# Order of the first four attention units on TensorE: own values, the next unit's scores, then the carried values, then transposes and k^T v

## Chip, cores, metric

One core of one Trainium2 chip. The metric is device time in microseconds (us); lower is better. Every time below is the median of several executions, with the range. Ratios are of means; where an interval holds 1, the ratio alone shows no difference.

Names: PE is TensorE's matmul, PEld its weight load, ACT ScalarE, DVE VectorE, POOL GpSimd, SP SyncE.

## The reference

Retention attention (scores with a decay, causal, without softmax) for 8 batches and 8 heads of 576 tokens and 64 dimensions, then a mixture of 4 experts over all 4608 tokens, mixed by given probabilities:

```python
scores = scale * np.matmul(q, k.transpose(0, 1, 3, 2))
ret = scores * Dmat[None]                 # gamma_h ** (i - j) for i >= j, else 0
attn = np.matmul(ret, v)                  # (8, 8, 576, 64) -> x (4608, 512)
for e in range(4):
    h = np.maximum(x @ w1[e], 0.0)
    out += p[:, e:e + 1] * (h @ w2[e])
```

The experts are nearly all of the work. Attention of batch 0 has to be done before the first expert product can start; attention of later batches is woven in between expert products.

## The kernel before

Batch 0 is cut into four units (two halves of the tokens, two groups of four heads). One unit goes through these steps; the comments give the names used below:

```python
class Unit:
    def trans_pe(self, between=0):      # "transposes": k and q on PE, then one copy to qkT on ACT
        for i, n in ((1, "k"), (0, "q")):
            if i == 0 and between:
                warm(between)           # "fillers": matmuls of zeros, 512 columns each
            ...                         # 4 transposes of 128 columns
        nc.scalar.activation(self.qk..., pt..., Copy)
    def scores(self):                   # 16 matmuls of a quarter of the array (64 x 64),
        ...                             # then one product with the triangle on DVE: sT
    def kv(self):                       # "k^T v": 16 or 24 small matmuls,
        ...                             # then two copies to sbd on ACT, 64 partitions each
    def values_own(self):               # 16 quarter-array matmuls of v and sT into o
        ...
    def values_carried(self):           # 2 or 4 matmuls of sbd and qkT, added into the same o,
        ...                             # then two copies to xt on ACT
```

The order in which they are issued (numbers in the text are the unit numbers u = 0 to 3):

```python
for u in range(NU):
    if u + 1 < NU:
        us[u + 1].cast(...)             # k and q on DVE, v on POOL; loads of w1 for u + 1 in (1, 2)
    if u < NU - 1:
        us[u].scores()
        if u == 0:
            warm(4)
        us[u + 1].trans_pe(2 if u == 0 else 1)
        us[u].kv()
    if u == 0:
        warm(1)
    us[u].values_own()
    if u == NU - 2:
        us[u + 1].scores()
        us[u + 1].kv()
        us[u].values_carried()
        warm(3)
    else:
        us[u].values_carried()
# ... cut: then the first expert's up products, ph = w1^T x, which read xt
```

Products that fill PSUM share a ring of four tiles, and in the traces PE's matmuls run in the order of the program.

## Time and profile before

| | before |
|---|---|
| time, 3 executions | 542.52 us (542.24 to 542.67) |
| span of the profiled execution | 540.9 us |
| PE busy | 532.8 us, 98% |
| carried values 0 start | 11.50 us |
| last xt copy ends | 21.60 us |

The page's first part of the kernel before gives busy us, the share of the span and the number of instructions of each engine:

```profile
PE 532.8 (98%) x4319; PEld 341.3 (63%) x4319; DVE 365.4 (68%) x484; ACT 112.1 (21%) x255; POOL 91.8 (17%) x126
```

PE is the engine to watch, and from 21.7 us on it has next to no gaps. So the only place where an order can matter is the stage before. The chain of waits of the kernel before (what the end was waiting for, read backwards; columns: start us, us, what), from carried values 0 (o L602) on:

```profile
11.50 0.29 PE o L602 x2
11.79 0.35 PE s L539 x16
12.13 0.33 PE pt L516 x4
12.46 0.21 PE w L140
12.68 0.24 PE pt L516 x4
...
13.00 1.02 ACT qkT L518
14.02 0.36 ACT sbd L577
...
14.83 0.34 PE o L602 x3
15.18 0.35 PE s L539 x16
...
16.39 1.03 ACT qkT L518
...
17.46 0.41 PE s L539 x13
17.87 0.07 issue
17.94 0.25 PE s L539 x3
18.19 1.09 PE kvp L558 x24
...
20.09 1.21 ACT xt L618 x3
...
21.34 2.84 PE ph L358 x12
```

It runs back and forth between PE and ACT, with a period of 3.39 us (the qkT copies at 13.00 and 16.39). The scores (s L539) of the next unit stand in every round although nothing in the round needs them. At the end there are four xt copies in a row on ACT, because carried values 2 were issued after k^T v 3.

### The profile page before, as it was taken

How to read it: one execution, taken by the hardware profiler on the slowest of the kernel's cores; microseconds unless marked ns; L12 is line 12 of the kernel's file. 1: busy time of each engine (PE TensorE's matmuls, PEld its weight loads, DVE VectorE, ACT ScalarE, POOL GpSimd, SP SyncE). 2: the span in 40 equal slices, each digit the busy share in tenths (PEclk: the TensorE clock that was granted, in tenths of full speed). 3: DMA queues.
4: the chain of work that ended last, by engine and by line, in shares of the span. 5: the costliest groups of instructions: out<-in, count | busy, mean ns of one | idle time of the engine just before them, and what ended most of it. 6: DMA issues, size and time to landing. Idle time of an engine off the chain costs nothing.

```text
span 540.9 us, 10332 instructions
## 1 busy us (share of the span) xinstructions
PE 532.8 (98%) x4319; PEld 341.3 (63%) x4319; DVE 365.4 (68%) x484; ACT 112.1 (21%) x255; POOL 91.8 (17%) x126
## 2 busy tenths in 40 slices
PE   8999999999999999999999999999999999999997
PEld 4544454568745884488547864687448844884486
DVE  5525669987488657876688648764886677557764
ACT  4623551122111220223022111131112200000010
POOL 5734002120211121211112111112111100010000
PEclk9999999999999999999999999999999999999999
DMA  9999947765265635655277517653654211110001
GB/s 237 208 209 249 229 121 187 142 160 121 82 117 131 154 92 98 139 116 142 67 155 131 147 55 135 150 140 90 99 135 118 75 49 39 41 41 21 0 26 54
DMA packets 145119, 63.56 MB, mean 118 GB/s; under 512 B 124240, under 2 KB 135888, under 8 KB 145072
## 3 DMA queue, kind: packets, MB, share of 16 engines
q1 hardware_dynamic: 134752, 43.50, 35.7%
q0 software_dynamic: 10176, 19.27, 16.3%
q8 instruction: 34, 0.56, 0.4%
q10 hardware_dynamic: 144, 0.13, 0.1%
q14 instruction: 13, 0.11, 0.1%
HBM read 53.56 MB, written 9.51 MB: 117 GB/s over the span
## 4 chain that ended last, share of the span: by engine, by line
PE 92%; DVE 4%; ACT 1%; DMA 1%; issue 0%; SPq 0%; DVEq 0%; ACTq 0%
PE ph L358 44%; PE pd L450 37%; PE po L377 4%; DVE h L364 2%; PE kvp L261 1%; PE s L274 1%; PE o L291 1%; ACT qkT L518 1%; DMA raw_0q<-in_q_dram 1%; PE pt L516 1%; PE o L284 1%; PE s L539 1%; DMA qkT<-bf_q 0%; DVE sT L541 0%; PE kvp L558 0%
## 5 line engine op out<-in xcount | busy, mean ns | idle before, releaser
L358 PE MATMUL ph<-xt,w 128*128 128x512 bf16 x1152 | 255.3, 379 | 1.3 <-DVE h L364 1.2
L358 PEld LDWEIGHTS <-w 128*128 128x128 bf16 x1152 | 110.8, 98 | 129.4 <-issue 1.7
L364 DVE SCALAR_TENSOR_TENSOR h<-ph,pB 128x1024 bf16<-128x1024 f32 x128 | 155.9, 1222 | 51.8 <-PE ph L358 51.6
L450 PEld LDWEIGHTS <-h 128*128 128x128 bf16 x1024 | 99.2, 98 | 14.1
L450 PEld LDWEIGHTS <-s 128*128 128x128 bf16 x768 | 74.7, 98 | 9.1
L450 PE MATMUL pd<-wx,h 128*128 128x256 bf16 x512 | 61.3, 273 | 0.0
L450 PE MATMUL pd<-wx,s 128*128 128x256 bf16 x512 | 61.2, 273 | 0.0
L222 POOL DMA_DIRECT2D pB<-pd x28 | 15.9, 568 | 169.5 <-DVE h L364 137.7
L266 ACT ACTIVATE sbd<-kvp 64x256 bf16<-64x256 f32 x48 | 18.2, 378 | 106.4 <-PE kvp L261 106.1
L485 POOL TENSOR_TENSOR ob<-v,p 128x256 f32<-128x256 f32 x15 | 10.9, 727 | 151.1 <-DVE v L482 99.1
L276 DVE TENSOR_TENSOR sT<-s,tri 128x1024 bf16<-128x1024 f32 x24 | 29.2, 1216 | 2.1 <-PE s L274 2.1
L450 PE MATMUL pd<-t4w,h 128*128 128x256 bf16 x256 | 30.6, 273 | 0.0
L450 PE MATMUL pd<-t2w,s 128*128 128x256 bf16 x256 | 30.6, 273 | 0.0
L450 PE MATMUL pd<-t3w,h 128*128 128x256 bf16 x256 | 30.6, 273 | 0.0
L467 DVE TENSOR_TENSOR u<-pd,p 128x256 f32<-128x256 f32 x16 | 6.8, 425 | 34.5 <-PE pd L450 34.5
L245 POOL TENSOR_TENSOR bf_q<-raw_q,gq 128x512 bf16<-128x512 f32 x24 | 25.7, 1070 | 23.4 <-DMA raw_q<-in_q_dram 16.8
L377 PE MATMUL po<-wx,h 128*128 128x512 bf16 x128 | 29.1, 379 | 0.1
L458 ACT ACTIVATE p<-pd 128x256 f32<-128x256 f32 x16 | 6.1, 384 | 94.9 <-PE pd L450 90.8
L469 DVE TENSOR_TENSOR oa<-pd,u 128x256 f32<-128x256 f32 x16 | 6.8, 424 | 23.7 <-PE pd L450 23.7
L431 DVE TENSOR_TENSOR s<-h,s 128x1024 bf16<-128x1024 bf16 x32 | 22.7, 748 | 0.0
L241 DVE TENSOR_TENSOR bf_k<-raw_k,gk 128x512 bf16<-128x512 f32 x24 | 21.9, 912 | 0.0
L249 ACT ACTIVATE bf_v<-raw_v 128x512 bf16<-128x512 f32 x24 | 15.1, 628 | 29.8 <-DMA raw_v<-in_v_dram 29.8
(147 smaller groups left out, 392.2 us busy)
## 6 DMA issues: line engine op xcount, KB each, us to landing
pB<-pd POOLq DMA_DIRECT2D x28, 256.0 KB, 3.9
raw_k<-in_k_dram SPq DMA_DIRECT2D x48, 128.0 KB, 2.8
raw_q<-in_q_dram SPq DMA_DIRECT2D x48, 128.0 KB, 3.1
raw_v<-in_v_dram SPq DMA_DIRECT2D x48, 128.0 KB, 3.8
wx<-in_moe_w_dram POOLq DMA_DIRECT2D x4, 1024.0 KB, 15.3
out_dram<-oa SPq DMA_DIRECT2D x16, 256.0 KB, 2.1
out_dram<-ob SPq DMA_DIRECT2D x15, 256.0 KB, 2.1
w<-in_moe_w_dram POOLq DMA_DIRECT2D x3, 1024.0 KB, 15.6
```

The costliest lines, as they stand in the source:

```text
L222: eng.dma_start(out=pB[t, e], in_=pd[e:e + 1, t * NT:(t + 1) * NT].to_broadcast([128, NT]))
L241: nc.vector.tensor_tensor(self.bf["k"], raw["k"], gk[:, :, 2 * p:2 * p + 2].unsqueeze(3).to_broadcast([128, NC, 2, D]), op=MULT)
L245: nc.gpsimd.tensor_tensor(self.bf["q"], raw["q"], gq[:, :, 2 * p:2 * p + 2].unsqueeze(3).to_broadcast([128, NC, 2, D]), op=MULT)
L249: nc.scalar.activation(self.bf[n], raw[n], Copy)
L266: nc.scalar.activation(sbd[r, self.p, :, r], kvp[r, :, :], Copy)
L276: nc.vector.tensor_tensor(self.sT[:, :, :, :].rearrange("p j c t -> p (j c) t"), s[:, :, :, :].rearrange("p j c t -> p (j c) t"), tri[:, : ...
L358: nc.tensor.matmul(ph[:, f, :], lhsT=w1_sb[e][:, dc, fc * 128:(fc + 1) * 128], rhs=x[:, dc, :], start=(dc == 0), stop=(dc == NDC - 1))
L364: nc.vector.scalar_tensor_tensor(h[:, fk:fk + 2, :], ph, 0.0, pB[t, e][:, :].unsqueeze(1).to_broadcast([128, 2, NT]), op0=MAX, op1=MULT)
L377: nc.tensor.matmul(po[:, g, :], lhsT=h[:, e * NFC + fc, ns * 128:(ns + 1) * 128], rhs=wx[e // 2][:, (e % 2) * NFC + fc, :, :].rearrange("p ...
L431: nc.vector.tensor_tensor(self.alloc("s4")[:, l], h[:, r, self.a], self.s2[:, l], op=SUB)
L450: mm = nc.tensor.matmul(dst, lhsT=src[:, kk, tok], rhs=rhs(c), start=(start and c == 0), stop=(c == KH - 1), skip_group_check=True)
L485: nc.gpsimd.tensor_tensor(self.ob[:, HF:Dm], self.v, self.p5, op=ADD)
```

## The change

The intent: PE waits for the sbd copies ahead of each carried values. Put the next unit's scores, which are ready, into that wait, and start the transposes right after the carried values. One filler less is issued at the end.

```diff
+    cast_unit(1)
+    us[0].scores()
+    warm(4)
+    us[1].trans_pe(2)
+    us[0].kv()
+    warm(1)
     for u in range(NU):
-        ... (the loop shown above)
+        if u + 2 < NU:
+            cast_unit(u + 2)
+        us[u].values_own()
+        if u + 1 < NU:
+            us[u + 1].scores()
+        us[u].values_carried()
+        if u + 2 < NU:
+            us[u + 2].trans_pe(1)
+        if u + 1 < NU:
+            us[u + 1].kv()
         if u == NU - 2:
-            us[u + 1].scores()
-            us[u + 1].kv()
-            us[u].values_carried()
-            warm(3)
-        else:
-            us[u].values_carried()
+            warm(2)
```

So there are two parts: the scores move into the wait (units 0 and 1), and carried values 2 move ahead of k^T v 3 (the tail).

## The prediction

> **What bounds the kernel.** The page gives TensorE (PE) 532.8 of 540.9 us busy (98%). The timeline shows PE with almost no gap from 21.7 us to the end. What idles lies before that, where four units (quarters of batch 0) go round PE and ScalarE (ACT) before the first expert product (ph). The chain of waits there has a cycle of 3.39 us per unit: qkT copy on ACT 1.02, two sbd copies on ACT 0.76, carried values on PE 0.34, next unit's scores 0.35, transposes with one filler 0.78, hand-overs 0.14 (qkT 2 starts at 13.00, qkT 3 at 16.39). After the last copy (ends 17.42): scores 3, k^T v 3 (18.19 to 19.28), sbd copies (19.30 to 20.07), and then four xt copies on ACT to 21.60, two of them unit 2's, whose carried values stand behind unit 3's k^T v. ph starts at 20.64 but has to wait for the third and fourth xt copy (21.34, 21.65).

> **What the change does.** One filler matmul of 0.21 us goes, nothing is added. In the built programs VectorE, GpSimd and DMA keep their order; ACT swaps only unit 2's xt copies with unit 3's sbd copies. On PE the scores of unit u+1 move ahead of the carried values of u, into time in which PE waits for the sbd copies: 0.31 us before carried 0 and 0.36 before carried 1.

> **Costed on the chain.**
> 1. Scores (0.35) leave the cycle: carried 0 stays at 11.50, qkT 2 starts at about 12.65 (was 13.00), qkT 3 at about 15.7 (was 16.39). xt 0 and xt 1 (0.77) just fit beside the transposes (0.78).
> 2. Between qkT 3 and k^T v 3 there is now a wait for sbd 2 (0.76) and carried 2, where before there were slow scores 3 (0.73). That gives back 0.25: k^T v 3 starts at about 17.75 (was 18.19), sbd 3 at 18.85.
> 3. xt 2 is done by then (17.8 to 18.6). The tail after sbd 3 is carried 3 (0.34) plus two xt copies (0.77), with hand-overs 1.2, against four copies, 1.5, before. Gain 0.3.
> Sum: last xt copy at about 20.85 against 21.60, 0.75 us earlier. PE is dense from there on, so most of it should last.

> **What could take it back.** The first half of w2 landed at about 26.6 (GpSimd's wait that ended at 26.61); the first down product, which needs it, began at 27.9 and would begin at about 27.1: 0.5 us of slack is left. The clock: [...] (512-column fillers 0.43 us apart at first, 0.21 from 5.9 us on). I expect no gap over 0.45 us, so no slow-down from the missing filler.

> **Prediction.** 542.52 - 0.75 = about 541.8 us, 0.14% faster; 8 in 10: 541.3 to 542.4. Faster by over 2%: 0.005; within 2%: 0.99; slower: 0.005.

> **What shows it right or wrong.** qkT 2 and 3 starting 0.35 and 0.7 us earlier; k^T v 3 at about 17.75; PE waiting for sbd before carried 2; two, not four, xt copies at the end; ph dense from about 20.9; then the down product at 27.1. Wrong if PE is late on another wait (scores 3 then slow again), if VectorE's scores products (1.22 us each) come to bind own values.

## The result, and the profile after

541.54 us (541.31 to 541.59, 4 executions) against 542.54 us (542.24 to 542.67, 4 executions): 1.0 us, or 0.18%, less. The ratio of the kernels is 0.9982, 95% interval 0.9964 to 0.9999. (A ratio is the mean time of one kernel's executions over that of the other's in the same rounds, so not quite the ratio of the medians.) By the measure of 2% that is the same. A second set, c_after below, gave 541.50 us (541.25 to 542.74, 5 executions) against 542.45 us.

The page's first part of the changed kernel, and the groups of the ph matmuls, before and then after:

```profile
PE 528.9 (98%) x4278; PEld 340.8 (63%) x4318; DVE 366.4 (68%) x484; ACT 112.3 (21%) x255; POOL 92.8 (17%) x126
```

```profile
L358 PE MATMUL ph<-xt,w 128*128 128x512 bf16 x1152 | 255.3, 379 | 1.3 <-DVE h L364 1.2
```

```profile
L358 PE MATMUL ph<-xt,w 128*128 128x512 bf16 x1118 | 252.5, 379 | 3.3 <-DVE h L364 1.4
```

Do not read the fall of PE's busy time, 3.9 us, as the gain. The programs have the same 1152 ph matmuls, but this trace holds records of only 1118; only one filler was really removed (PEld: 4319 to 4318). The chain of waits of the changed kernel shows the stage itself:

```profile
11.09 0.30 PE o L602 x2
...
11.41 0.69 ACT xt L618 x2
...
12.15 1.02 ACT qkT L518
13.18 0.36 ACT sbd L577
...
13.99 0.35 PE o L602 x3
...
14.36 0.68 ACT xt L618 x2
...
15.09 1.03 ACT qkT L518
...
16.16 0.41 PE s L539 x13
16.57 0.48 issue
17.05 0.25 PE s L539 x3
17.30 0.22 PE o L602 x2
17.52 1.07 PE kvp L558 x24
...
19.84 0.47 ACT xt L618
...
20.34 3.71 PE ph L358 x16
```

The scores are gone from the round, whose period is now 2.94 us (12.15 to 15.09). The transposes have left the chain as well: the xt copies on ACT, which run beside them, now end last. At the end two xt copies are left instead of four. ph goes on at 20.34 us instead of 21.34. Two things in this trace are not what the change does:

- Carried values 0 start at 11.09 instead of 11.50 us, and up to own values 0 the two programs are the same; carried values 0 wait for the sbd copies, which do not depend on the scores now issued in between. So 0.41 of the 1.0 us between the traces was there before the change begins.
- The pause inside scores 3 is longer: 0.48 us on the chain, where the kernel before had 0.07.

### The profile page after: what moved, and what is told of

The parts are those of the page before. It is cut to its first block, busy times and chain, and to the rows that moved or that the text cites. A ratio compares the mean times of both kernels' runs of the same rounds, so it can differ in the third digit from the quotient of the medians. Undisturbed runs are those within 1.5% of the kernel's fastest.

```text
span 539.9 us, 10290 instructions
## 1 busy us (share of the span) xinstructions
PE 528.9 (98%) x4278; PEld 340.8 (63%) x4318; DVE 366.4 (68%) x484; ACT 112.3 (21%) x255; POOL 92.8 (17%) x126
## 3 DMA queue, kind: packets, MB, share of 16 engines
HBM read 53.56 MB, written 9.51 MB: 117 GB/s over the span
## 4 chain that ended last, share of the span: by engine, by line
PE 92%; DVE 4%; ACT 1%; issue 1%; DMA 1%; SPq 0%; DVEq 0%
PE ph L358 45%; PE pd L450 37%; PE po L377 4%; DVE h L364 2%; PE kvp L261 1%; PE s L274 1%; PE o L291 1%; ACT qkT L518 1%; DMA raw_0q<-in_q_dram 1%; PE o L284 1%; DVE sT L541 0%; PE kvp L558 0%; PE pt L516 0%; PE s L539 0%; PE o L602 0%
## 5 line engine op out<-in xcount | busy, mean ns | idle before, releaser
L358 PE MATMUL ph<-xt,w 128*128 128x512 bf16 x1118 | 252.5, 379 | 3.3 <-DVE h L364 1.4
L485 POOL TENSOR_TENSOR ob<-v,p 128x256 f32<-128x256 f32 x15 | 10.9, 727 | 146.9 <-DVE v L482 97.6
L245 POOL TENSOR_TENSOR bf_q<-raw_q,gq 128x512 bf16<-128x512 f32 x24 | 26.6, 1108 | 27.0 <-DMA raw_q<-in_q_dram 15.1
L429 DVE TENSOR_TENSOR h<-h 128x1024 bf16<-128x1024 bf16 x32 | 22.2, 735 | 0.0
```

Of the source, the lines that this page charges most:

```text
L245: nc.gpsimd.tensor_tensor(self.bf["q"], raw["q"], gq[:, :, 2 * p:2 * p + 2].unsqueeze(3).to_broadcast([128, NC, 2, D]), op=MULT)
L358: nc.tensor.matmul(ph[:, f, :], lhsT=w1_sb[e][:, dc, fc * 128:(fc + 1) * 128], rhs=x[:, dc, :], start=(dc == 0), stop=(dc == NDC - 1))
L429: nc.vector.tensor_tensor(h[:, l, self.b], h[:, l, self.a], h[:, l, self.b], op=SUB)
L485: nc.gpsimd.tensor_tensor(self.ob[:, HF:Dm], self.v, self.p5, op=ADD)
```

## The experiments

All times stand beside executions of the kernel before on the same chip. The table has what each trace shows: when PE reached full rate (by the clock record of the trace; the profile's clock column does not show this first change: it stands at 1.00 while fillers of 512 columns are still 0.43 us apart), when carried values 0 start, when the last xt copy ends, the difference of the two, which I call the stage, how far apart the two scores 3 matmuls are between which the pause falls (other neighbours in scores 3: at most 0.07 us), and the time of the profiled execution.

| trace | full rate from | carried 0 starts | last xt copy ends | stage | pause in scores 3 | time |
|---|---|---|---|---|---|---|
| before | 6.39 | 11.50 | 21.60 | 10.10 | 0.29 | 542.67 |
| c_before | 6.17 | 11.71 | 21.60 | 9.89 | 0.09 | 542.70 |
| after | 4.07 | 11.09 | 20.60 | 9.51 | 0.70 | 541.59 |
| c_after | 4.68 | 11.24 | 21.53 | 10.29, half clock from 18.3 | 0.56 | 542.74 |
| e_scores | 6.72 | 11.41 | 20.30 | 8.89 | none | 541.31 |
| e_tail | 5.00 | 11.42 | 21.41 | 9.99 | 0.10 | 542.85 |
| e_more | 5.27 | 11.29 | 20.37 | 9.08 | none | 541.45 |
| e_less | 4.08 | 11.01 | 22.25 | 11.24, half clock from 10.9 | none | 543.43 |
| e_split | 6.92 | 11.37 | 20.07 | 8.70 | 0.42 | 541.30 |
| e_nofill | 4.72 | 11.54 | 20.58 | 9.04, half clock from 18.4 | 0.17 | 543.10 |
| e_gap | 7.09 | 11.40 | 21.07 | 9.67 | 0.65 | 542.06 |
| e_pos | 4.03 | 11.10 | 20.18 | 9.08 | 0.19 | 541.16 |
| e_best | 7.00 | 11.24 | 20.30 | 9.06 | 0.56 | 541.52 |
| e_final | 4.03 | 11.63 | 19.91 | 8.28 | none | 541.13 |

In all rows but one the time is the end of the last xt copy plus 521.0 to 521.4 us (the exception, e_nofill, still runs at half clock when ph starts). So what is won or lost by 21 us is kept to the end, and the stage is all that has to be explained.

### Two controls: c_before and c_after

The two kernels again, unchanged, to see what differs between executions of one and the same program.

> Control: the kernel before, unchanged. All theories: within 0.3 us of the kernel before. Theory A (0.6 us of the 1.0 us gain belong to the new order; 0.4 us that the two traces differ by before carried values 0 is scatter of the start: when PE reached full rate and when the first q landed): over further traces the start of carried values 0 scatters between about 11.0 and 11.5 us for one and the same kernel, and copies of one kernel differ by up to 0.4 us. Rival B (the whole 1.0 us belongs to the change): this trace again has carried values 0 at 11.5.

> The changed kernel again, on the chip of the other runs. Theory A: 0.6 to 1.0 us below before, carried values 0 anywhere between 11.0 and 11.5 us, and the last xt copy 9.5 us after its start (10.1 in the kernel before). Rival B: 1.0 us below before and carried values 0 at 11.1 again.

c_before: 542.46 us (542.15 to 542.70) against 542.45 us, ratio 1.0001 (0.9989 to 1.0014). c_after: 541.50 us (541.25 to 542.74), ratio 0.9990 (0.9977 to 1.0002); one of its five executions, the profiled one, is at 542.74, and one at 542.03.

The start of carried values 0 does scatter: 11.01 to 11.71 us over all 14 traces, 11.09 to 11.71 over these two kernels, where the code up to there is the same. One part of it can be seen: the fillers at the start are 0.43 us apart until PE reaches full rate and 0.21 after, and that moment falls anywhere between 4.0 and 7.1 us; unit 0's transposes are slow or fast accordingly (four of them took 0.61 us in the kernel before, 0.40 in c_after). It does not explain all (e_final has an early one and the second latest carried values 0). Theory A, that the trace difference of 1.0 us is part change and part start, holds. But the start has no reason to favour one kernel over several executions, and the medians differ by 0.95 to 1.0 us in both sets. That suggests a stage that is on the average shorter than the first trace shows, and the pause in scores 3 is where the next runs found room.

### The two parts alone: e_scores and e_tail

```diff
 # e_scores: the changed kernel, with the old tail for unit 2
+        if u == NU - 2:
+            us[u + 1].kv()
+            us[u].values_carried()
+            warm(3)
+            continue
         us[u].values_carried()
 ...
```

```diff
 # e_tail: the kernel before, with the new tail for unit 2
             us[u + 1].scores()
-            us[u + 1].kv()
             us[u].values_carried()
-            warm(3)
+            us[u + 1].kv()
+            warm(2)
```

> New order for units 0 and 1 alone; unit 2 keeps the old tail (k^T v 3 ahead of carried values 2, three fillers, four xt copies at the end). If scores in the hand-over are the main part: qkT copy 3 starts 4.0 us after carried values 0, as in the changed kernel (4.9 before), the last xt copy ends about 9.65 us after it, and the time is 0.4 to 0.5 us below before, 0.1 to 0.2 above the changed kernel. If the tail is the main part: less than 0.2 below before.

> Old order for units 0 and 1, unit 2 with the new tail (carried values 2 ahead of k^T v 3, two fillers). qkT copy 3 starts 4.9 us after carried values 0 as before; k^T v 3 is later by about 0.25 as it now waits for the sbd copies 2 and carried values 2, which eats most of what two instead of four xt copies at the end give: the last xt copy ends about 10.0 after carried values 0, the time 0.1 us below before (0 to 0.2). If the tail is the main part: 0.3 or more below before.

e_scores: 541.67 us (541.31 to 543.13) against 542.45 us, ratio 0.9994 (0.9981 to 1.0008). One execution at 543.13 (clock 1.000, cause open) pulls its mean up; the other four, 541.31 to 541.70, lie below all nine of the kernel before (541.90 to 542.72). e_tail: 542.36 us (541.95 to 542.85), ratio 1.0001 (0.9989 to 1.0014). So the scores part carries the gain, and the tail part has none that can be measured: with nearly the same pause the stage of e_tail is 9.99 us and that of c_before 9.89. Its qkT copy 3 starts 4.89 us after carried values 0, as expected; that of e_scores 3.98, as expected too, but the last xt copy ends 8.89 us after carried values 0 instead of the expected 9.65. The end of the chain of waits of e_scores shows why:

```profile
15.39 1.03 ACT qkT L518
...
16.47 0.42 PE s L539 x16
16.89 1.09 PE kvp L558 x24
...
18.79 1.21 ACT xt L618 x3
...
20.05 4.13 PE ph L358 x18
```

k^T v 3 follows scores 3 at once, 0.47 us after the end of the qkT copy (16.42 to 16.89). With the new tail it has to wait for the sbd copies 2 and carried values 2; in e_more below, which has the new tail and no pause either, k^T v 3 starts 0.99 us after that copy (16.30 to 17.29), 0.52 later:

```profile
17.01 0.29 PE o L602 x2
17.29 1.07 PE kvp L558 x24
```

From there to the end of the last xt copy the new tail is quicker, 3.08 instead of 3.41 us. By these two traces the net is a loss of 0.19: stages 9.08 and 8.89.

### The pause in scores 3: e_more, e_less, e_pos

The scores of e_scores run through, those of the changed kernel stop after 13 of 16 in both traces. Nothing in the program makes the fourteenth matmul wait. The windows of the changed kernel for the matmuls that write or read s (stretch: length, PE busy, count, clock, DMA share, GB/s):

```profile
16.15:16.50 0.35, 0.34 (x13) 1.00 1.26 209
16.50:16.70 0.20, 0.07 (x5) 1.00 1.36 230
16.70:17.04 0.34, 0.00 (x0) 1.00 1.21 199
17.04:17.30 0.26, 0.25 (x3) 1.00 1.30 215
```

The trace has a DMA queue named instruction, q8, with 34 packets of 16 KB; from the third on they begin 254 PE instructions apart on the average, so I take them for blocks of PE's instructions. Count PE's matmuls and weight loads, and the semaphore instructions that the traces hold among them, from the first filler on. In the changed kernel scores 3 begin at row 421; the fourteenth weight load, row 447, still runs before the stop, and the fourteenth matmul, row 448, waits. In the kernel before one semaphore instruction more stands ahead (at 15.2 us), and there the fourteenth weight load waits too: row 448 again. In the DMA view of the changed kernel for 14.6 to 15.7 us there is one such packet (queue: packets, MB, share):

```profile
q8 instruction: 1, 0.02, 5.1%
```

It is the first of 16 KB in this execution; it begins at about 14.7 us and is over at about 15.6. If PE runs out of instructions there (theory F), the stop must move with the number of instructions ahead of it, not with what they do:

```diff
 # e_more: the same PE time in 8 more instructions, early
-    warm(4)
+    w = ring_tile("w", [128, 512])
+    for i in range(8):
+        nc.tensor.matmul(w[:, 0:256], lhsT=zz[:, 0:128], rhs=zz[:, 0:256], start=True, stop=True)
```

```diff
 # e_less: 14 instructions fewer, early
-    warm(4)
-    us[1].trans_pe(2)
+    us[1].trans_pe()
     us[0].kv()
-    warm(1)
```

```diff
 # e_pos: the filler between unit 3's transposes as four of 128 columns: 6 more
-            us[u + 2].trans_pe(1)
+            us[u + 2].trans_pe(1, 4 if u == 1 else 1)
 ...   # cut: trans_pe and warm take the number of pieces
```

> The changed kernel with the four early fillers of 512 columns as eight of 256: the same PE time, 8 more instructions ahead of scores 3. In the changed kernel scores 3 stop for 0.35 to 0.48 us after 13 of 16 matmuls. Theory F ([...]a packet of 16 KB on the instruction queue begins 2.4 us before the stop ends in both traces): the stop moves 4 matmuls forward, to after 9 of 16; the time stays within 0.3 us of the changed kernel. Rival S (a semaphore, the qkT write, or what the matmul reads): the stop stays after 13.

> The changed kernel without the four, two and one fillers round unit 0's scores and k^T v: 14 instructions fewer ahead of scores 3. Theory F: no stop within scores 3 (0.42 us in all); the block's end now falls 7 matmuls later, before the third matmul of k^T v 3, where 0 to 0.4 us may be waited; the time 0 to 0.3 us below the changed kernel if the granted clock holds. Rival S: scores 3 still stop after 13 matmuls. Clock: if these fillers keep the clock up, transposes of unit 1 or 2 take 0.6 instead of 0.4 us and the time is over 1 us above the changed kernel; if they do not, no difference.

> The changed kernel with the filler between unit 3's transposes cut into four of 128 columns: the same PE time[...]. Theory F: scores 3 may now stop after 10 of 16 (not 13), until 2.3 to 2.4 us after the packet on the instruction queue began; if the packet came early (over 2.5 us before the tenth matmul) no stop. Rival S: a stop after 13. Time within 0.3 us of the changed kernel at full clock.

e_more: 541.63 us (541.30 to 542.32) against 542.16, ratio 0.9993 (0.9980 to 1.0007). It shows no stop at all, against the expectation, so it does not tell where one would be; its packet began at 13.4 us, over 3 us before the matmul in question. e_less: 543.29 us (542.46 to 543.43), ratio 1.0017 (1.0004 to 1.0030), for another reason, below; no stop in scores 3, as expected, but its packet began 5 us ahead, so this tells little. e_pos: 541.34 us (541.16 to 542.14) against 542.29, ratio 0.9986 (0.9974 to 0.9998). Its scores 3, which begin at row 427, stop after 10 of 16, as expected: the eleventh matmul is row 448 again. The windows of e_pos, for the same matmuls; a stretch also counts those that began in the one before and still run:

```profile
16.15:16.42 0.27, 0.26 (x10) 1.00 1.27 213
16.42:16.56 0.14, 0.14 (x11) 1.00 1.29 211
16.56:16.70 0.14, 0.14 (x6) 1.00 1.22 196
```

Theory S, a semaphore or the data, falls: the same matmul of the same unit passes in one kernel and stops in the other, and six instructions moved the stop by three matmuls. e_nofill below, with four fewer, moved it to after 14, where 15 was expected; but its trace holds two semaphore instructions ahead of scores 3 (13.14 and 15.68 us) where the changed kernel has none, and with them counted the matmul that waits is row 448 too. So it is in all ten traces with a stop, whatever stands there. In these ten the later matmul starts 2.2 to 2.4 us after the packet began; in the four without, row 448 was due 2.4 us or more after it (2.45 in e_scores, 2.6 in e_final). So the pause is best read as the time by which the block was late; place and time say so, and no run changed the fetch itself. The packet's start in turn varied from 13.4 to 15.8 us among the traces. What starts it, and why at such different times, was not tried.

This bears on the question of the controls: with a pause of 0.70 us the changed kernel's stage is 9.5 us, and about 9.1 without one (e_more) or with one of 0.19 (e_pos, where carried values 2 still wait for the sbd copies anyway), against 9.9 to 10.1 before. Both traces of the changed kernel itself have a pause; how many of its other executions had one is not known.

### The clock: e_less again, e_nofill, e_gap

c_after's profiled execution was at 542.74. The windows of c_after, cut at the changes of its clock (columns: stretch, its length, busy us of PE, PEld, DVE, ACT, POOL with counts, granted clock, DMA share, GB/s):

```profile
14.92:18.33 3.41, 2.96 (x75) 1.93 (x72) 1.64 (x2) 2.72 (x7) 3.09 (x10) 1.00 1.29 208
18.33:21.75 3.42, 3.06 (x32) 1.58 (x30) 3.08 (x25) 1.52 (x4) 3.36 (x7) 0.50 1.24 207
21.75:25.16 3.41, 3.41 (x17) 1.57 (x16) 0.00 (x0) 1.40 (x2) 2.23 (x4) 1.00 1.20 201
```

For exactly one stretch of 3.41 us PE ran at half rate (granted clock 0.50). It began 13.65 us, four times that length, after PE had reached full rate (4.68 us); I call such stretches, counted on from full rate, windows. The window ahead of the drop was not idle: PE is busy for 2.96 of its 3.41 us, 87%. e_less did it for two windows, 6.83 us (10.9 to 17.7), after one that PE was 68% busy, and with that lost 1.1 us on the kernel before (543.29 against 542.16); all five of its executions have a mean clock of 0.992 to 0.995. So the early fillers are needed.

Both windows ahead of a drop held no filler, so I tried that as the rule:

```diff
 # e_nofill: no fillers between the transposes of units 2 and 3, none after k^T v 3
-            us[u + 2].trans_pe(1)
+            us[u + 2].trans_pe()
-        if u == NU - 2:
-            warm(2)
```

```diff
 # e_gap: one filler more, ahead of carried values 2
             us[u + 1].scores()
+        if u == NU - 2:
+            warm(1)
         us[u].values_carried()
```

> The changed kernel without the fillers between the transposes of units 2 and 3 and without the two after k^T v 3: from 10.3 us to the first ph at 19.5 us no filler of 512 columns is left. So far the granted clock fell to half exactly where one whole window of 3.41 us, counted on from the moment PE reached full rate, held no filler (one trace of the changed kernel, one without the early fillers); small matmuls alone, though they show PE 87% busy, did not keep it. Theory K (fillers keep the clock, not the busy share): every execution now has at least one such window, the trace shows half clock for one window or more before 22 us, and all runs are at 542.2 us or more, 0.7 us and more above the changed kernel. Rival B (busy share counts): full clock in most runs, and 541.2 us or less, as two fillers fewer are on the way. The stop in scores 3, if any, comes 2 matmuls later, after 15 of 16.

> The changed kernel with one filler more, between scores 3 and carried values 2, where PE waits. The longest stretch without filler falls from 3.8 us to under 2.5, less than a window. Theory K: no run with half clock after the start, all runs within 541.2 to 541.8; median as the changed kernel's, as the filler lies in a wait. Rival: slow runs (542 us and over) as often as in the changed kernel (2 of 9), or the median 0.2 us higher.

e_nofill: 542.79 us (541.05 to 544.28, 6 executions) against 542.29, ratio 1.0008 (0.9994 to 1.0022). Five of six took 542.26 or more; four of these have a mean clock of 0.996 or 0.997, as one window of half clock gives (c_after: 0.996), and the trace shows one such window. The longest, 544.28, has 1.000 and stays unexplained. But one execution, at 541.05, was faster than any of the changed kernel; and in the trace the window from 11.55 to 14.96 us held no filler and kept the clock. So the rule as I wrote it is wrong. e_gap: 541.61 us (541.39 to 542.06), ratio 0.9990 (0.9978 to 1.0002), no window at half clock in its trace, though two of five were at 542.05 and 542.06, over the 541.8 of the expectation. The one of these that was profiled has the full clock, a late start (carried 0 at 11.40) and a pause of 0.65: the filler, meant for a wait, lay behind the pause and delayed the rest.

Scores and own values use a quarter of the array at a time (64*64 in the traces, where fillers have 128*128), so PE can be nearly always busy and yet lightly used. In the kernel before the windows are 46% and more; the new order, with its pause, comes down to 39% in the first trace and 31% in c_after, depending on where the window falls. By this estimate that would be a price of the new order: it is nearer to the 30 to 33% at which the clock fell. The record agrees as far as so few executions can: a mean clock of 0.997 or less stands in three of 34 executions of the changed kernel and of its variants that keep its early fillers and those between the transposes (e_more, e_split, e_gap, e_pos, e_best), and in none of 45 of the kernel before.

Slow executions are not all of this kind. In the last set the kernel before had two of 11 over 543.4 us, with mean granted clocks of 1.000 and 0.999, one of e_final's six was at 542.40 with 1.000, and c_after's second long execution (542.03) has 1.000, where a window at half rate would make 0.997 (an estimate: half of 3.41 us, of 540 us). What those are is open.

### Shorter tails: e_split, e_best, e_final

After k^T v 3 the stage is a chain of copies: two sbd copies, carried values 3, two xt copies. DVE then prepares only the mixing weights of the experts, which the program issues after these copies.

```diff
 # e_split: the changed kernel; unit 3's copies shared by ACT and DVE, one filler for two
+                elif j == 1 and self.split:
+                    y = nc.vector.tensor_copy(dst, kvp[jr])               # sbd: 64 partitions each
 ...
+                    y.append(nc.vector.tensor_copy(dst, src) if a else nc.scalar.activation(dst, src, Copy))
 ...
-            warm(2)
+            warm(1)
 # e_best: e_split with e_gap's filler
 # e_final: e_scores, with unit 3's sbd and xt copies and unit 2's xt copies shared, warm(1) for warm(3)
```

The sbd copies are divided by partitions and the xt copies by banks; no other division was tried. All three kernels gave right results.

> The changed kernel with unit 3's two sbd copies and its xt copies each shared between ACT and VectorE (by partitions, and by banks), and one filler instead of two after k^T v 3. If the tail after k^T v 3 is a chain of copies as I read it (two sbd copies 0.77, carried values 3 0.34, two xt copies 0.76): each pair takes half, the first ph matmul that waits for xt starts about 1.9 us after k^T v 3 starts plus 1.1, that is 0.6 us sooner after k^T v 3 than in the changed kernel, and the time is 0.5 to 0.75 us below the changed kernel (about 540.9) in runs at full clock. If something else ends that stage (fillers, own values 3): less than 0.2.

> Shared copies of unit 3 (as in e_split) and the filler of e_gap. At full clock the stage from carried values 0 to the first ph that waits takes 8.7 us as in e_split, 0.6 to 0.8 less than in the changed kernel, and no run falls to half clock: all runs 540.7 to 541.4, median about 541.1, 0.3 to 0.5 us below the changed kernel. If the clock was not the cause of e_split's two slower runs (541.84, 542.77): again one or two runs over 541.7.

> The version that the runs point to: scores in the hand-over for units 0 and 1 (as in e_scores), the old place of k^T v 3 ahead of carried values 2, and the copies after it (sbd 3, xt 2, xt 3) each shared between ACT and VectorE, one filler. If the tail is a chain of copies: the last xt copy ends 1.65 us after the end of k^T v 3's matmuls (2.4 in e_scores, 2.0 in the changed kernel), that is about 8.1 us after carried values 0 began if scores 3 do not stop, 8.1 to 8.7 with a stop; the changed kernel shows 9.5. The time is 540.5 to 541.0 at full clock, 0.5 to 1.0 below the changed kernel. If weights bind next, the first down product waits for w2 (landed 25.7 to 26.6 so far), and half of that gain is lost.

e_split: 541.32 us (541.30 to 542.77) against 542.16, ratio 0.9991 (0.9978 to 1.0003). Its stage is 8.70 with a pause of 0.42, 0.8 less than the changed kernel's with 0.70; but its start was at 11.37, and the time of three executions at 541.3 is not the 540.9 that I expected. e_best: 541.52 us (541.26 to 542.97), ratio 0.9996 (0.9983 to 1.0009), two of five over 542.5; the filler did not prevent that, and the expectation missed. The one at 542.97 has a mean clock of 0.996, so the filler did not keep the clock there; the one at 542.60 has 1.000, so its cause is another. e_final: 541.08 us (540.60 to 542.40, 6 executions) against 542.39 us (542.27 to 543.79, 11 executions), ratio 0.9975 (0.9962 to 0.9988). The end of its chain of waits:

```profile
17.11 1.07 PE kvp L560 x24
18.18 0.22 PE o L607 x2
18.39 0.23 PE w L140
...
18.67 0.42 PE o L597 x16
19.09 0.34 PE o L607 x4
...
19.45 0.47 ACT xt L618
...
19.96 4.06 PE ph L358 x18
```

Its stage is 8.28 us, expected 8.1 to 8.7, though the median is 0.1 above what I had expected; carried values 0 started at 11.63 in this trace, the second latest of all. It has only the useful half of the change, and is 1.3 us below the kernel before, where the changed kernel was 0.95 to 1.0 below in its own sets. The two were not run side by side, so that it beats the changed kernel is likely and not shown.

## Why the prediction was right, point by point

- **The size and the place: right.** 541.54 us against 541.8, within the range. The gain arose before the first ph, and was kept to the end: time less the end of the last xt copy is 521.07 us before and 520.99 after. That the sum came so near is in part luck. The prediction added 0.70 (round), -0.25 (given back ahead of k^T v 3) and 0.30 (tail); the first pair of traces shows 0.89, -0.63 and 0.33, together 0.59, and the 0.41 from the start came on top.
- **Scores leave the round: right, and somewhat undersized.** Measured from the start of carried values 0, the qkT copies 2 and 3 start 0.44 and 0.89 us earlier (1.50 to 1.06, 4.89 to 4.00), where the prediction had 0.35 and 0.7. The xt copies beside the transposes, called a fit of 0.77 and 0.78, became the longer path.
- **"That gives back 0.25": right in kind, wrong in its cause.** The prediction took the slow scores 3 (0.73 us) of the first trace for a property of the kernel. By the reading above they are a late block of instructions: 0.09 to 0.29 us in three traces with the old order, none to 0.70 with the new. k^T v 3 started 0.26 us earlier by the first trace (6.69 to 6.43 after carried values 0), not 0.44, and 0.69 earlier in e_more, where there was no pause.
- **The tail, 0.3: right for itself.** From k^T v 3 to the end of the last xt copy 3.41 became 3.08 us. But its cost ahead of k^T v 3, 0.52 us against e_scores, is larger, so this part of the change gains nothing. The prediction's own terms (0.25 against 0.3) already had it near zero.
- **0.75 against 1.0 us.** In the first pair of traces 0.59 belong to the stage and 0.41 to the start. How the 1.0 us between the medians divides among the scores' part, the length of the pause and the scatter of the start is not settled, as each kernel left one or two traces.
- **What could take it back.** The first down product started at 26.91 us, expected 27.1, and did not wait for w2. The fillers' full rate, put at 5.9 us, began at about 6.4. The clock: "no slow-down from the missing filler" held in the first four executions; in the second set the profiled one of five fell to half rate, without a single gap over 0.6 us before it. The prediction took the lack of gaps over 0.45 us for enough, which no trace had shown; by this one it is not.

## What to carry to other kernels

Where two engines hand work to each other in turns, write down the period and move out of it whatever the period does not need; here that gave about 0.45 us a round, and a second reordering that only exchanged one wait for another gave nothing. A pause between equal instructions that wait for nothing may be the instruction stream itself (here up to 0.70 us): change the number of instructions ahead of it and see whether it moves. Take several traces of one program before reading tenths of a microsecond out of a pair. Look at the granted clock of every execution, not only at PE's busy share: here PE was 87% busy in the window before it lost half of its clock, and taking the early fillers out cost 1.1 us.
